# Batch 1 masked by bias products, six half loads, three up products in two parts, and a new instruction order

## The chip, the cores and the metric

The kernel runs on one NeuronCore of one Trainium2 chip. The metric is the device time of one execution in microseconds; seven runs of the kernel before gave a median of 255.86 us (255.72 to 255.92). One further execution was profiled, and every duration below comes from that one.

## The reference, cut to what matters

```python
# q, k, v: 8 batches x 8 heads x 576 positions x 64
rel = pos[:, None] - pos[None, :]
mask_plain = (rel >= 0) & (rel < 32)                        # heads 0 to 3
mask_dil = (rel >= 0) & (rel < 128) & (rel % 4 == 0)        # heads 4 to 7
attn = softmax(where(mask, q @ k.T / 8, -1e9))
x = (attn @ v), heads side by side: 4608 tokens x 512
h = ((x @ w1) * (x @ w2)) @ w3                              # 512 -> 1024 -> 1024
out = h @ w_out                                             # 1024 -> 512, fp32
```

## The kernel before, in words

**Stages.** Each batch is 576 tokens. Attention works on blocks of 96 queries by 128 keys, for four heads at once: a batch has 12 blocks, six for each half of the heads (u = 0 and u = 1). Tokens are kept in the order of their residue modulo 4, so that a dilated window becomes a band too. After attention come, for units of 288 tokens (two per batch, 16 in all), eight pairs of up products (w1 and w2), their elementwise product, and for every 128 tokens a down product with wf = w3 @ w_out, which the kernel computes once.

**Names of the steps.** The kernel puts every step on a list under a name, with the engine, a guessed duration, what it depends on and a rank. The names are used throughout, with batch and part as numbers:

- T: stream transposes on VectorE (DVE) that turn the loaded rows of q, k and v. VT: TensorE transposes of v back to rows (line 403). VK: their copy out of PSUM into the v tile vp (lines 413 and 415).
- S: the score matmuls of one group of blocks (line 445). E: the exp of the group on ScalarE (ACT, line 456). M: its two multiplications by the 0/1 mask on DVE (line 464).
- V: the product with v (line 481) for three blocks, V0.0 to V0.3 in batch 0. R and N: reciprocal and normalisation on DVE (lines 492 and 504). X: TensorE transposes of the result (line 521). K: the copy of X into XT, the operand of the up products (line 529).
- W3T, W3C, W3M, W3D: transpose of a w3 tile (line 638), its copy (645), its product with w_out (650), and the copy into wf (661 and 663).
- A and B: up products with w1 and w2, four matmuls each (line 553). CA: copy of A on ACT (564). G: the product A times B on DVE (569). Y and CY: down product (580) and its copy (591).

**Two ways to mask.** A plain group holds five blocks (40 score matmuls), and its exp is multiplied by the mask afterwards. A biased group holds three blocks: four matmuls of 288 columns (line 428) first write a bias of 0 or -30000 into PSUM, 24 score matmuls add to it, and no M follows. In the kernel before only batch 0 is biased (`BIASED = 1`).

**The order.** The function Plan.run plays the list through with the guessed durations and issues each engine's instructions in the order so found; on the chip nothing is reordered afterwards. Among ready steps of one engine the lowest rank goes first; RANK (FIRST for batch 0) gives the ranks by kind. FIRST_LOADS is the order of the loads after batch 0's, `ON_DVE` names the copies that go to DVE instead of ACT, and LEAD says how far attention runs ahead of the ups. Until the first up product, wherever the plan has no work for TensorE, it puts a filler in: a matmul of 256 columns on zeros (line 692). WARM such matmuls, of 512 columns in the kernel before, stand at the very start (line 675).

**PSUM.** It is used as eight banks. A group of scores takes four (0 to 3 or 4 to 7), a V two, everything else one. A step may start on a bank once the readers of what was there have ended.

**Loads.** q and k of batch 0, u = 0, come whole through SyncE's queue and are rounded on ACT (line 271). All other loads convert to bf16 and are issued by GpSimd (POOL) in one list: rows of q, k and v (line 245), w1 and w2 in three column parts (line 303), w_out (309), w3 (318). At most eight of them are under way, so each issue from the ninth on waits for the landing of the one eight places before. The five mask instructions on POOL (line 358) stand in the same list.

Of the kernel before, what the change touches and what calls it, by code (L numbers as in the profile page):

```python
# [10 lines left out]
P = 128  # L11
BF16 = mybir.dt.bfloat16
F32 = mybir.dt.float32
U32 = mybir.dt.uint32
AL = mybir.AluOpType
# [4 lines left out]
S = 576  # L20
# [8 lines left out]
BIG = 30000.0  # L29
BIASED = 1  # L30
LATE = False
# [3 lines left out]
RES = (0, 2, 1, 3)  # L35
RANK = dict(E=0.4, VK=2, K=0.3, N=1.5, T=3, VT=0.3, S=0.4, V=0.05, X=0.2, W=6, C=-1)
FIRST = {"E": 2, "VK": 0.4, "K": 0.5, "N": 0.2, "T": 2, "VT": 0.05, "S": 0.2, "V": 0.05, "X": 0.4}
WARM = 14
FILL = 110
FIRST_LOADS = ("30", "31", "w0", "w1", "32", "w2", "o0", "o1", "q1", "k1", "33", "34", "v1", "35", "36", "37")  # L40
SHIFT = {}
ON_DVE = ("VK0.0.1", "VK1.0.1", "W3D1", "W3D3", "W3D7")
GRP = 5
WHOLE = ("qn", "kn")
BUSY = 4500
LEAD = 1.1

# [12 lines left out]
class Plan:  # L60
# [15 lines left out]
    def run(self):  # L76
        fills = []
        users = {id(t): [] for t in self.tasks}
# [40 lines left out]
        while len(order) < n:  # L119
            progress = True  # L120
            while progress:
                progress = False
                for e in engines:
# [21 lines left out]
                    if e == "DMA":  # L145
                        free[e] = now + t.dur[0]
                        if t.dur[1]:
                            dma = max(dma, now + t.dur[0]) + t.dur[1]
                            t.end = dma + 1900
                        else:  # L150
                            t.end = free[e]
                    else:
                        t.end = free[e] = now + t.dur
                        if e == "SP" and t.name[0] == "X" and dma > now:
                            t.end = free[e] = now + t.dur + BUSY
                            dma += 1.5 * t.dur
# [23 lines left out]
def kernel(  # L180
# [48 lines left out]
    vts = [const.tile([P, 2, PADK + S, 2], BF16, name=f"vt{i}") for i in range(1)]  # L229
    warm = const.tile([P, 512], BF16, name="warm")  # L230

# [122 lines left out]

    def masks_of_bias():

        for at, first, n in ((0, 0, 4), (4, 1, 2), (6, 4, 3), (9, 4, 3), (12, 0, 4)):
            nc.gpsimd.tensor_scalar(
                out=mask[:, at : at + n, :],
                in0=bias[:, first : first + n, :],  # L360
                scalar1=0.0,
                scalar2=None,
                op0=AL.is_ge,
            )

# [41 lines left out]

    def v_keep(b, u, half, eng):
        dst = vps[b % 2][:, 4 * u : 4 * u + 4, 3 * half : 3 * half + 3, 0:D]
        o = dst.rearrange("p h m (j c) -> p m h j c", c=2)  # L410
        i = spread[(b, u, half)].rearrange("p m c (h j) -> p m h j c", h=4)
        if eng == "ACT":
            nc.scalar.copy(out=o, in_=i)
        else:
            nc.vector.tensor_copy(out=o, in_=i)
# [50 lines left out]
    class Step:  # L466
# [59 lines left out]

        def keep(self, eng):
            if eng == "ACT":
                nc.scalar.copy(out=self.cols(), in_=self.x)
            else:  # L530
                nc.vector.tensor_copy(out=self.cols(), in_=self.x)

# [16 lines left out]

    def up(k, f, w_sb, key):  # L550
        o = bank(UNIT)
        for j, c in enumerate(ORDER):
            nc.tensor.matmul(  # L553
                out=o,
                lhsT=w_sb[:, c, f * P : (f + 1) * P],
                rhs=unit_cols(k, c),
                start=(j == 0),
                stop=(j == DCH - 1),
            )
        held[(key, k, f)] = o  # L560

# [110 lines left out]
    def warm_up():  # L672
        o = bank(512)
        for i in range(WARM):
            nc.tensor.matmul(out=o, lhsT=warm[:, 0:P], rhs=warm, start=True, stop=True)
# [15 lines left out]
    def fill():  # L691
        nc.tensor.matmul(out=bank(256), lhsT=warm[:, 0:P], rhs=warm[:, 0:256], start=True, stop=True)  # L692

# [3 lines left out]
    c0 = add("const2", "DVE", 1400, [c1], constants, -98)  # L697
    add("warm", "PE", 700 + 427 * WARM, [c1], warm_up, 0)

# [45 lines left out]
    plan.dma = 1200 + 1350 * len(WHOLE)  # L745
    for u in range(2):
        for nm in ("qn", "kn", "vn"):
            if u or nm not in WHOLE:
                loads_rows(nm, 0, (u,))
    idt = add("ident", "DMA", (600, 0), [], lambda: make_identity(nc, ident), 2.5, lat=150)  # L750
    bnd = add("band", "DMA", (800, 0), [c1], band, 1.5, lat=150)
    blk = add("blocks", "ACT", 1200, [bnd], blocks, -5, lat=100)
    blk = add("no halo", "DVE", 150, [blk], no_halo, 0, lat=80)
    mk = add("masks", "DMA", (2500, 0), [blk], masks_of_bias, 26.5, lat=150)
    lw12 = {}
    for x in FIRST_LOADS:
# [9 lines left out]
        else:  # L766
            loads_rows(x[0] + "n", c)

# [14 lines left out]
    kept, paced = {}, []  # L783
    prev = {"x": [None] * 4}
    readers, grp_of, todo, n_grp, steps = {}, {}, [], 0, 0
# [24 lines left out]
    for b in range(B):  # L810
# [9 lines left out]
        for u in range(2):  # L820
# [3 lines left out]
            for half in range(2):  # L824
# [3 lines left out]
                if (b, u, half) == (0, 1, 1):  # L828
                    late.append(x)
                name = f"VK{b}.{u}.{half}"  # L830
                eng, dur = ("DVE", 980) if name in ON_DVE else ("ACT", 880)
                vals[(b, u, half)] = [
                    add(name, eng, dur, [x, c0], lambda b=b, u=u, h=half, e=eng: v_keep(b, u, h, e),
                        10 * b + rank("VK", b), lat=100)
                ]
        if b >= DIRECT_V:
# [7 lines left out]
        def group(blocks, biased):  # L844
# [11 lines left out]
            else:  # L856
# [4 lines left out]
                ms = [  # L861
                    add(f"M{n}.{h}", "DVE", 150 + 100 * g.n, [e, mk], lambda h=h: g.masks(h),
                        10 * b + 2, lat=80)
# [21 lines left out]
        while steps < 4 * B:  # L885
# [18 lines left out]
            rc = add(f"R{n}", "DVE", 240, [vv], st.recip, 10 * bb + rank("N", bb), lat=0,  # L904
                     after=[prev["x"][i]])
            ns = [
# [4 lines left out]
            if bb < TURNED:  # L911
                x = add("X" + n, "PE", 310, ns + [idt], st.back, bb - 99 + rank("X", bb), slot=1)
                name = f"K{n}"
                eng, dur = ("DVE", 460) if name in ON_DVE else ("ACT", 640)
                x = add(name, eng, dur, [x], lambda st=st, eng=eng: st.keep(eng),
                        10 * bb + rank("K", bb), lat=100)
            else:
                x = add("XD" + n, "SP", 1300, ns, st.back_dma, 0, lat=1200)
            kept.setdefault(bb, []).append(x)
            prev["x"][i] = x  # L920
            vdone.setdefault(bb, []).append(vv)

# [94 lines left out]
```

## Time and profile before

| | |
|---|---|
| median of 7 runs | 255.86 us |
| the profiled execution | 255.84 us |
| its span in the profile | 254.1 us |
| TensorE busy | 246.8 us (97%), 2763 matmuls |
| DVE busy | 165.5 us (65%) |
| ACT busy | 126.2 us (50%) |
| POOL busy | 66.5 us (26%) |
| fillers | 37, first at 6.8 us, last at 21.4 us |
| granted TensorE clock | 1.00 in every stage asked for |

The span is the time from the first instruction to the last; the 1.7 us between it and the execution's time lie around it. A busy TensorE counts fillers and warm-up as busy. Matmuls overlap, so that the listed duration of one (286 ns for 288 columns) is longer than what it costs; the distance between two starts (about 122 ns) is the cost. Where the text speaks of a wait of TensorE, it means that the next matmul in its fixed order was not yet ready.

### The profile page before, as it was taken

How to read it: one execution, taken by the hardware profiler on the slowest of the kernel's cores; microseconds unless marked ns; L12 is line 12 of the kernel's file. 1: busy time of each engine (PE TensorE's matmuls, PEld its weight loads, DVE VectorE, ACT ScalarE, POOL GpSimd, SP SyncE). 2: the span in 40 equal slices, each digit the busy share in tenths (PEclk: the TensorE clock that was granted, in tenths of full speed). 3: DMA queues.
4: the chain of work that ended last, by engine and by line, in shares of the span. 5: the costliest groups of instructions: out<-in, count | busy, mean ns of one | idle time of the engine just before them, and what ended most of it. 6: DMA issues, size and time to landing. Idle time of an engine off the chain costs nothing.

```text
span 254.1 us, 6809 instructions
## 1 busy us (share of the span) xinstructions
PE 246.8 (97%) x2763; PEld 170.1 (67%) x2763; DVE 165.5 (65%) x342; ACT 126.2 (50%) x221; POOL 66.5 (26%) x103
## 2 busy tenths in 40 slices
PE   7799999999999999999999999999999999999994
PEld 2588766565777666667676766776767666777662
DVE  3983547799889898678767886837737365333321
ACT  5677333986635534463636626356353553333331
POOL 7653129643622712008160310700000000000000
PEclk9999999999999999999999999999999999999999
DMA  7999999999999999828999658852332222311114
GB/s 225 207 199 206 207 211 210 209 103 189 185 136 182 205 186 171 193 67 140 167 143 160 95 72 106 120 100 67 67 65 67 66 68 67 102 33 56 42 41 124
DMA packets 59374, 33.40 MB, mean 131 GB/s; under 512 B 44752, under 2 KB 49232, under 8 KB 59344
## 3 DMA queue, kind: packets, MB, share of 16 engines
q0 software_dynamic: 38544, 18.81, 58.2%
q1 hardware_dynamic: 20656, 14.10, 23.2%
q8 instruction: 21, 0.34, 0.6%
q14 instruction: 9, 0.07, 0.1%
q10 hardware_dynamic: 144, 0.07, 0.1%
HBM read 38.80 MB, written 9.44 MB: 190 GB/s over the span
## 4 chain that ended last, share of the span: by engine, by line
PE 93%; ACT 3%; DMA 2%; DVE 1%; issue 0%; ACTq 0%
PE ps L553 50%; PE ps L580 24%; PE ps L650 5%; PE ps L481 4%; PE ps L445 4%; DMA gt<-in_q_dram 2%; ACT et L456 2%; PE ps L692 2%; PE ps L638 1%; PE ps L403 1%; PE ps L521 1%; ACT w3T L645 1%; PE ps L598 1%; DVE qt L394 1%; ACT qn L271 0%; DVE kt L379 0%
## 5 line engine op out<-in xcount | busy, mean ns | idle before, releaser
L553 PE MATMUL ps<-XT,w_sb 128*128 128x288 bf16 x1024 | 136.2, 286 | 0.0
L553 PEld LDWEIGHTS <-w_sb 128*128 128x128 bf16 x1024 | 97.8, 98 | 30.6
L569 DVE TENSOR_TENSOR gt<-ps,asb 128x288 bf16<-128x288 f32 x128 | 57.6, 454 | 52.0 <-PE ps L553 49.8
L564 ACT CAST asb<-ps 128x288 bf16<-128x288 f32 x128 | 51.1, 400 | 51.7 <-PE ps L553 49.4
L580 PE MATMUL ps<-wf_sb,gt 128*128 128x512 bf16 x280 | 65.8, 379 | 0.0
L591 ACT COPY osb<-ps 128x512 f32<-128x512 f32 x35 | 20.5, 587 | 56.3 <-PE ps L580 56.3
L580 PEld LDWEIGHTS <-gt 128*128 128x128 bf16 x280 | 27.4, 98 | 26.9
L293 POOL DMA_DIRECT2D vp<-in_v_dram x48 | 30.0, 635 | 38.3 <-PE ps L481 21.7
L456 ACT ACTIVATE et<-ps 128x1920 bf16<-128x1920 f32 (+2 forms) x21 | 34.2, 1635 | 5.5 <-PE ps L445 4.9
L504 DVE TENSOR_TENSOR xo<-ps,rcp 96x384 bf16<-96x384 f32 (+1 forms) x48 | 31.5, 676 | 0.6
L464 DVE TENSOR_TENSOR et<-et,mask 128x960 bf16<-128x960 bf16 (+1 forms) x34 | 21.4, 645 | 4.9 <-ACT et L456 4.7
L394 DVE STREAM_TRANSPOSE qt<-qn 128x320 uint32<-128x320 uint32 (+3 forms) x34 | 22.4, 669 | 2.1 <-ACT qn L271 1.8
L481 PEld LDWEIGHTS <-et 128*128 128x128 bf16 x384 | 14.3, 98 | 1.7
L481 PE MATMUL ps<-vp,et 128*128 128x65 bf16 x384 | 15.1, 193 | 0.0
L650 PE MATMUL ps<-wo_sb,w3T 128*128 128x512 bf16 x64 | 14.8, 379 | 0.1
L394 DVE STREAM_TRANSPOSE kt<-kn 128x320 uint32<-128x320 uint32 (+3 forms) x18 | 11.6, 642 | 4.4 <-PE ps L445 4.3
L492 DVE RECIPROCAL rcp<-ps 96x12 f32<-96x12 f32 x32 | 6.8, 215 | 10.5 <-PE ps L481 10.2
L245 POOL DMA_DIRECT2D kn<-in_k_dram x8 | 5.5, 686 | 30.4 <-DVE kt L394 18.4
L445 PEld LDWEIGHTS <-kt 32*128 32x128 bf16 x768 | 9.1, 92 | 6.3 <-issue 4.5
L445 PE MATMUL ps<-qt,kt 32*128 32x96 bf16 x768 | 12.1, 201 | 1.2 <-DVE kt L379 1.2
L379 DVE STREAM_TRANSPOSE kt<-kn 128x576 uint32<-128x576 uint32 (+1 forms) x9 | 9.9, 1121 | 1.4 <-PE ps L445 1.4
L650 PEld LDWEIGHTS <-w3T 128*128 128x128 bf16 x64 | 5.9, 98 | 6.8 <-ACT w3T L645 0.6
(55 smaller groups left out, 119.1 us busy)
## 6 DMA issues: line engine op xcount, KB each, us to landing
qn<-in_q_dram POOLq DMA_DIRECT2D x7, 576.0 KB, 8.1
kn<-in_k_dram POOLq DMA_DIRECT2D x7, 576.0 KB, 7.4
w3n<-in_moe_w_dram POOLq DMA_DIRECT2D x8, 256.0 KB, 15.1
out_dram<-osb SPq DMA_DIRECT2D x7, 256.0 KB, 2.5
out_dram<-osb SPq DMA_DIRECT2D x8, 224.0 KB, 2.9
vp<-in_v_dram POOLq DMA_DIRECT2D x6, 288.0 KB, 9.8
out_dram<-osb SPq DMA_DIRECT2D x8, 192.0 KB, 2.7
out_dram<-osb SPq DMA_DIRECT2D x8, 160.0 KB, 3.5
```

The source lines that it names most:

```text
L293: nc.gpsimd.dma_start(out=vp[32 + p0 : 32 + p0 + n, 4:8, m, 0:D], in_=v_rows(b, 4, 4 * t0 + res, [[4 * D, n], [S * D, 4], [1, D]]),)
L394: nc.vector.transpose(out=o, in_=i)
L445: nc.tensor.matmul(out=self.sp[:, g, QB * i : QB * i + QB], lhsT=kt[prt, u, QB * m : QB * m + P, c], rhs=qq, start=(c == 0 and not biased) ...
L456: nc.scalar.activation(out=ev, in_=self.sp[:, :, 0:x], func=ACT.Exp, scale=scale)
L464: nc.vector.tensor_tensor(out=ev, in0=ev, in1=mk, op=AL.mult)
L481: nc.tensor.matmul(out=self.o[:, g, mm, :], lhsT=grp.et[:, c0 : c0 + P], rhs=vps[self.b % 2][:, 4 * self.u + g, 3 * self.hf + mm, 0 : D + ...
L504: nc.vector.tensor_tensor(out=dst, in0=self.o[0:QB, hs, :, 0:D], in1=self.rcp[0:QB, hs, :].unsqueeze(3).to_broadcast([QB, n, 3, D]), op=AL ...
L553: nc.tensor.matmul(out=o, lhsT=w_sb[:, c, f * P : (f + 1) * P], rhs=unit_cols(k, c), start=(j == 0), stop=(j == DCH - 1),)
L564: nc.scalar.copy(out=a_sb, in_=held[("a", k, f)])
L569: nc.vector.tensor_tensor(out=gt[:, f, c0 : c0 + UNIT].rearrange("p (r m t) -> p m r t", r=2, m=BLK), in0=held[("b", k, f)].rearrange("p ( ...
L580: nc.tensor.matmul(out=y, lhsT=gt[:, f, c0 : c0 + P], rhs=wf_sb[:, f, :], start=(f == 0), stop=(f == KFF - 1),)
L650: nc.tensor.matmul(out=o, lhsT=w3T[ft][:, g, :], rhs=wo_sb[:, g, :], start=(g == 0), stop=(g == KFF - 1),)
```

## The change

- Batch 1 is biased too (`BIASED = 2`): its blocks form four groups of three with bias products, and have no mask multiplications. The groups of five begin with batch 2.
- Batch 1's q, k and v are loaded in two halves each (u = 0, u = 1), six loads for three, at new places in FIRST_LOADS. Batch 0's four loads on POOL get their own order (B0_LOADS), and w1 and w2 come ahead of most of w3.
- The first three up products (A0.0, B0.0, A0.1) are two tasks each: the two matmuls on the first heads' half (XT0), and later the two on the second (XT1).
- Six copies (HALVED: K1.0, K1.1, VK0.0.0, VK1.0.1, VK1.1.0, VK1.1.1) are two instructions, half on ACT and half on DVE. Some other copies move between the two engines (ON_DVE).
- The mask instructions are five tasks at an earlier place in POOL's list.
- The warm-up is 28 matmuls of 256 columns for 14 of 512.
- Ranks and LEAD have new values, and the plan's model of the loads knows of the limit of eight. By these the instruction order of every engine changes in most places; the number of instructions changes little: TensorE gets 16 bias matmuls more and 17 fillers fewer (20 for 37), DVE four mask multiplications fewer.

The new order on TensorE, by the names above, from the start to the first ups (each V, S and VT as a whole; "p" is the first part of an up product):

```
warm-up, filler, S0.0, S0.1, filler, VT0.0 (both halves), 7 fillers, V0.0, S0.2, VT0.1.0,
3 fillers, X0.0, V0.1, filler, S0.3, 4 fillers, V0.2, X0.1, VT0.1.1, W3T0, 2 fillers,
A0.0p, X0.2, B0.0p, filler, V0.3, A0.0, A0.1p, B0.0, A0.1, B0.1, A0.2, ...
```

and in batch 1's stage:

```
A1.7, W3M0, W3T2, W3M1, W3T3, W3M2, VT1.0, W3T4, W3M3, W3M4, S1.0, S1.1, V1.0, W3T5, B1.7, V1.1,
VT1.1, W3T6, W3M5, X1.0, W3T7, W3M6, S1.2, S1.3, V1.2, X1.1, W3M7, V1.3, X1.2, Y0, S2.0, X1.3, A2.0, ...
```

The diff, cut to its core:

```diff
 BIG = 30000.0
-BIASED = 1
+BIASED = 2
 LATE = False
 TURNED = 2
 DIRECT_V = 2
 ORDER = (2, 3, 0, 1)
 RES = (0, 2, 1, 3)
-RANK = dict(E=0.4, VK=2, K=0.3, N=1.5, T=3, VT=0.3, S=0.4, V=0.05, X=0.2, W=6, C=-1)
-FIRST = {"E": 2, "VK": 0.4, "K": 0.5, "N": 0.2, "T": 2, "VT": 0.05, "S": 0.2, "V": 0.05, "X": 0.4}
-WARM = 14
+RANK = dict(E=0.2, VK=0.2, K=1, N=1, T=0.3, VT=0.05, S=0.4, V=0.2, X=0.4, W=0.5, C=5)
+FIRST = {"E": 0.5, "VK": 0.2, "K": 3, "N": 0.3, "T": 1.5, "VT": 0.05, "S": 0.3, "V": 0.2, "X": 0.05}
+WARM = 28
 FILL = 110
-FIRST_LOADS = ("30", "31", "w0", "w1", "32", "w2", "o0", "o1", "q1", "k1", "33", "34", "v1", "35", "36", "37")
+FIRST_LOADS = ("w0", "30", "w1", "w2", "o0", "31", "o1", "32", "33", "v10", "34", "q10", "k10", "q11", "35", "v11", "36", "k11", "37")
 SHIFT = {}
-ON_DVE = ("VK0.0.1", "VK1.0.1", "W3D1", "W3D3", "W3D7")
+ON_DVE = ("K0.2", "K1.0", "K1.1", "K1.3", "VK1.0.1", "VK1.1.0", "W3D0", "W3D3", "W3D4", "W3D6")
 GRP = 5
 WHOLE = ("qn", "kn")
+B0_LOADS = ("k1", "v0", "q1", "v1")
+HALVED = ("K1.0", "K1.1", "VK0.0.0", "VK1.0.1", "VK1.1.0", "VK1.1.1")
+MASK_AT = 19.5
+PARTED = 3
 BUSY = 4500
-LEAD = 1.1
+LEAD = 1.3
 
...
                         if t.dur[1]:
-                            dma = max(dma, now + t.dur[0]) + t.dur[1]
+                            if len(landed) >= 8:
+                                free[e] = max(now, landed[-8]) + t.dur[0]
+                            dma = max(dma, free[e]) + t.dur[1]
                             t.end = dma + 1900
+                            landed.append(t.end)
                         else:
...
 
-    def masks_of_bias():
-
-        for at, first, n in ((0, 0, 4), (4, 1, 2), (6, 4, 3), (9, 4, 3), (12, 0, 4)):
-            nc.gpsimd.tensor_scalar(
-                out=mask[:, at : at + n, :],
-                in0=bias[:, first : first + n, :],
-                scalar1=0.0,
-                scalar2=None,
-                op0=AL.is_ge,
-            )
+    MASKS = ((0, 0, 4), (4, 1, 2), (6, 4, 3), (9, 4, 3), (12, 0, 4))
+
+    def mask_of_bias(i):
+
+        at, first, n = MASKS[i]
+        nc.gpsimd.tensor_scalar(
+            out=mask[:, at : at + n, :],
+            in0=bias[:, first : first + n, :],
+            scalar1=0.0,
+            scalar2=None,
+            op0=AL.is_ge,
+        )
 
...
 
-    def v_keep(b, u, half, eng):
+    def v_keep(b, u, half, eng, hs=slice(0, 4)):
         dst = vps[b % 2][:, 4 * u : 4 * u + 4, 3 * half : 3 * half + 3, 0:D]
-        o = dst.rearrange("p h m (j c) -> p m h j c", c=2)
-        i = spread[(b, u, half)].rearrange("p m c (h j) -> p m h j c", h=4)
+        o = dst.rearrange("p h m (j c) -> p m h j c", c=2)[:, :, hs, :, :]
+        i = spread[(b, u, half)].rearrange("p m c (h j) -> p m h j c", h=4)[:, :, hs, :, :]
         if eng == "ACT":
...
 
-        def keep(self, eng):
+        def keep(self, eng, c=slice(0, 6 * QB)):
             if eng == "ACT":
-                nc.scalar.copy(out=self.cols(), in_=self.x)
+                nc.scalar.copy(out=self.cols()[:, c], in_=self.x[:, c])
             else:
-                nc.vector.tensor_copy(out=self.cols(), in_=self.x)
+                nc.vector.tensor_copy(out=self.cols()[:, c], in_=self.x[:, c])
 
...
 
-    def up(k, f, w_sb, key):
-        o = bank(UNIT)
-        for j, c in enumerate(ORDER):
+    def up(k, f, key, chunks=ORDER, first=True, last=True):
+        if first:
+            held[(key, k, f)] = bank(UNIT)
+        for j, c in enumerate(chunks):
             nc.tensor.matmul(
-                out=o,
-                lhsT=w_sb[:, c, f * P : (f + 1) * P],
+                out=held[(key, k, f)],
+                lhsT={"a": w1_sb, "b": w2_sb}[key][:, c, f * P : (f + 1) * P],
                 rhs=unit_cols(k, c),
-                start=(j == 0),
-                stop=(j == DCH - 1),
+                start=(first and j == 0),
+                stop=(last and j == len(chunks) - 1),
             )
-        held[(key, k, f)] = o
 
...
     def warm_up():
-        o = bank(512)
+        o = bank(256)
         for i in range(WARM):
...
     def fill():
-        nc.tensor.matmul(out=bank(256), lhsT=warm[:, 0:P], rhs=warm[:, 0:256], start=True, stop=True)
+        nc.tensor.matmul(out=bank(256), lhsT=warm[:, 0:P], rhs=warm, start=True, stop=True)
 
     plan.fill, plan.fill_from = fill, 2000
 
     c1 = add("const", "DVE", 1200, [], first_constants, -99)
     c0 = add("const2", "DVE", 1400, [c1], constants, -98)
-    add("warm", "PE", 700 + 427 * WARM, [c1], warm_up, 0)
+    add("warm", "PE", 700 + 213 * WARM, [c1], warm_up, 0)
 
...
     plan.dma = 1200 + 1350 * len(WHOLE)
-    for u in range(2):
-        for nm in ("qn", "kn", "vn"):
-            if u or nm not in WHOLE:
-                loads_rows(nm, 0, (u,))
+    for x in B0_LOADS:
+        loads_rows(x[0] + "n", 0, (int(x[1]),))
     idt = add("ident", "DMA", (600, 0), [], lambda: make_identity(nc, ident), 2.5, lat=150)
     bnd = add("band", "DMA", (800, 0), [c1], band, 1.5, lat=150)
     blk = add("blocks", "ACT", 1200, [bnd], blocks, -5, lat=100)
     blk = add("no halo", "DVE", 150, [blk], no_halo, 0, lat=80)
-    mk = add("masks", "DMA", (2500, 0), [blk], masks_of_bias, 26.5, lat=150)
+    mk = [
+        add(f"masks{i}", "DMA", (x, 0), [blk], lambda i=i: mask_of_bias(i), MASK_AT + 0.1 * i,
+            lat=150)
+        for i, x in enumerate((1200, 710, 940, 940, 1200))
+    ]
     lw12 = {}
...
         else:
-            loads_rows(x[0] + "n", c)
+            loads_rows(x[0] + "n", c, (int(x[2]),) if x[2:] else None)
 
...
                 eng, dur = ("DVE", 980) if name in ON_DVE else ("ACT", 880)
+                ways = [(eng, dur, slice(0, 4))]
+                if name in HALVED:
+                    ways = [("ACT", 540, slice(0, 2)), ("DVE", 560, slice(2, 4))]
                 vals[(b, u, half)] = [
-                    add(name, eng, dur, [x, c0], lambda b=b, u=u, h=half, e=eng: v_keep(b, u, h, e),
+                    add(name, e, dur, [x, c0],
+                        lambda b=b, u=u, h=half, e=e, hs=hs: v_keep(b, u, h, e, hs),
                         10 * b + rank("VK", b), lat=100)
+                    for e, dur, hs in ways
                 ]
...
                 eng, dur = ("DVE", 460) if name in ON_DVE else ("ACT", 640)
-                x = add(name, eng, dur, [x], lambda st=st, eng=eng: st.keep(eng),
+                ways = [(eng, dur, slice(0, 6 * QB))]
+                if name in HALVED:
+                    ways = [("ACT", 400, slice(0, 3 * QB)), ("DVE", 270, slice(3 * QB, 6 * QB))]
+                x = [
+                    add(name, e, dur, [x], lambda st=st, e=e, c=c: st.keep(e, c),
                         10 * bb + rank("K", bb), lat=100)
+                    for e, dur, c in ways
+                ]
             else:
-                x = add("XD" + n, "SP", 1300, ns, st.back_dma, 0, lat=1200)
+                x = [add("XD" + n, "SP", 1300, ns, st.back_dma, 0, lat=1200)]
             kept.setdefault(bb, []).append(x)
             prev["x"][i] = x
             vdone.setdefault(bb, []).append(vv)
 
-    seq = 10
+    seq, parted = 20, 0
     G, Y, gates, stores, pairs = {}, {}, [], [], []
 
     def ups(k, f):
         nonlocal seq
         b, hf = k // 2, k % 2
-        need = kept[b][0:2] + kept[b][2 + hf : 3 + hf]
+        plain = kept[b][0] + kept[b][1]
+        need = plain + kept[b][2 + hf]
         wl = lw12[(0, 0, 1, 1, 2, 2, 2, 2)[f]]
         lap = k * UNIT - RING
         free = [Y[i] for i in range(max(0, lap // P), (lap + UNIT - 1) // P + 1)]
-        seq += 1
-        a = add(f"A{k}.{f}", "PE", 490, need + wl, lambda: up(k, f, w1_sb, "a"), seq, slot=1,
-                after=free + pairs[-1:])
+
+        def product(key, after):
+
+            nonlocal seq, parted
+            name = f"{key.upper()}{k}.{f}"
+            seq += 1
+            if k or parted == PARTED:
+                return add(name, "PE", 490, need + wl, lambda: up(k, f, key), seq, slot=1,
+                           after=after), []
+            parted += 1
+            p = add(name + "p", "PE", 245, plain + wl,
+                    lambda: up(k, f, key, ORDER[2:], last=False), seq - 5, slot=1, after=after)
+            return add(name, "PE", 245, need + [p],
+                       lambda: up(k, f, key, ORDER[:2], first=False), seq), [p]
+
+        a, p = product("a", free + pairs[-1:])
         pairs.append(a)
-        ca = add("CA", "ACT", 400, [a], lambda: copy_a(k, f), -1, lat=100,
+        ca = add("CA", "ACT", 400, [a] + p, lambda: copy_a(k, f), -1, lat=100,
                  after=[gates[-6] if len(gates) > 5 else None])
-        seq += 1
-        bb = add(f"B{k}.{f}", "PE", 490, need + wl, lambda: up(k, f, w2_sb, "b"), seq,
-                 slot=1, after=[a])
-        G[(k, f)] = add("G", "DVE", 460, [bb, ca], lambda: gate(k, f), -1, lat=100)
+        bb, p = product("b", p or [a])
+        bb = [bb] + p
+        G[(k, f)] = add("G", "DVE", 460, bb + [ca], lambda: gate(k, f), -1, lat=100)
         gates.append(G[(k, f)])
```

More of the change, by code (lines that the diff above doesn't have):

```diff
@@ L76, in run @@
     def run(self):
-        fills = []
+        fills, landed = [], []
         users = {id(t): [] for t in self.tasks}
@@ L229 @@
     vts = [const.tile([P, 2, PADK + S, 2], BF16, name=f"vt{i}") for i in range(1)]
-    warm = const.tile([P, 512], BF16, name="warm")
+    warm = const.tile([P, 256], BF16, name="warm")
     def bank(n, dtype=F32):
@@ L783 @@
     kept, paced = {}, []
-    prev = {"x": [None] * 4}
+    prev = {"x": [[]] * 4}
     readers, grp_of, todo, n_grp, steps = {}, {}, [], 0, 0
@@ L861, in group @@
                 ms = [
-                    add(f"M{n}.{h}", "DVE", 150 + 100 * g.n, [e, mk], lambda h=h: g.masks(h),
+                    add(f"M{n}.{h}", "DVE", 150 + 100 * g.n, [e] + mk, lambda h=h: g.masks(h),
                         10 * b + 2, lat=80)
@@ L904 @@
             rc = add(f"R{n}", "DVE", 240, [vv], st.recip, 10 * bb + rank("N", bb), lat=0,
-                     after=[prev["x"][i]])
+                     after=prev["x"][i])
             ns = [
```

## The prediction

> **What bounds the kernel now.** I read the page first, then TensorE by stage, then its instructions in order of time.
>
> ```profile
> span 254.1 us, 6809 instructions
> PE 246.8 (97%) x2763; PEld 170.1 (67%) x2763; DVE 165.5 (65%) x342; ACT 126.2 (50%) x221; POOL 66.5 (26%) x103
> ```
>
> The busy time by stage (us from:to, length, then TensorE's busy time first):
>
> ```profile
> 0.00:6.90 6.90, 5.37 (x15) 2.03 (x16) 2.65 (x19) 4.11 (x9) 5.58 (x17) 1.00 0.76 224
> 6.90:21.70 14.80, 12.93 (x258) 10.81 (x257) 11.36 (x26) 10.67 (x14) 7.90 (x12) 1.00 1.25 203
> 21.70:61.70 40.00, 39.85 (x460) 27.60 (x459) 28.04 (x51) 24.35 (x38) 16.89 (x24) 1.00 1.20 188
> 61.70:250.40 188.70, 188.66 (x2036) 129.69 (x2034) 123.16 (x249) 86.84 (x162) 36.17 (x53) 1.00 0.72 111
> ```
>
> From 21.7 to 250.4 us TensorE stands still for 0.19 us in all. A DVE, ACT or DMA instruction saved there is worth nothing; a matmul added costs its time. What can be gained lies before 21.5 us, where much of "busy" is filler. The timeline (start, duration) of TensorE's last start-up steps:
>
> ```profile
> 15.84 0.43 PE L521 MATMUL ps<-ident,xo 96*128 96x96 bf16 x6
> 16.11 1.80 PE L692 MATMUL ps<-warm 128*128 128x256 bf16 x15
> 17.75 0.65 PE L428 MATMUL ps<-bias,ident 128*128 128x288 bf16 x4
> 18.33 0.44 PE L445 MATMUL ps<-qt,kt 32*128 32x96 bf16 x24
> 18.70 0.51 PE L403 MATMUL ps<-ident,vt 128*128 128x128 bf16 x6
> ...
> 19.31 1.80 PE L692 MATMUL ps<-warm 128*128 128x256 bf16 x15
> 20.95 0.53 PE L481 MATMUL ps<-vp,et 128*128 128x65 bf16 x12
> 21.32 0.38 PE L692 MATMUL ps<-warm 128*128 128x256 bf16 x2
> 21.53 1.63 PE L553 MATMUL ps<-XT,w_sb 128*128 128x288 bf16 x12
> ```
>
> Durations overlap; starts give the cost. A filler is 0.109 us (1.64/15); a biased score group 0.95 (17.75 to 18.70); the up products begin at 21.53. A group of five plain blocks costs 0.65: the four ups from 64.81 need 0.49 of the 1.14 to 65.95.
>
> ```profile
> 64.81 0.65 PE L553 MATMUL ps<-XT,w_sb 128*128 128x288 bf16 x4
> 65.40 0.62 PE L445 MATMUL ps<-qt,kt 32*128 32x96 bf16 x40
> 65.95 1.16 PE L553 MATMUL ps<-XT,w_sb 128*128 128x288 bf16 x8
> ```
>
> Loads land one by one; POOL's waits for the ninth and later issues show when:
>
> ```profile
> 7.88 0.75 POOL L303 DMA_DIRECT2D w_sb<-in_moe_w_dram  x1 [0.30 <-DMA vn<-in_v_dram]
> 9.37 0.74 POOL L303 DMA_DIRECT2D w_sb<-in_moe_w_dram  x1 [0.74 <-DMA qn<-in_q_dram]
> 10.76 0.54 POOL L318 DMA_DIRECT2D w3n<-in_moe_w_dram  x1 [0.64 <-DMA kn<-in_k_dram]
> 12.11 0.74 POOL L303 DMA_DIRECT2D w_sb<-in_moe_w_dram  x1 [0.81 <-DMA vn<-in_v_dram]
> ```
>
> So POOL's first four half loads land at about 7.9, 9.3, 10.7 and 12.0 us.
>
> **What the Trainium skill says.** "TensorE: Matmul & The Clock Gate", section "Wait — 56ns, not 53.3ns?": start to start N/2.4 GHz plus 2.5 ns when warm, N/1.2 GHz cold. The trace agrees: 16 ups in 1.96 us are 122.5 ns for N=288, and the first warm-up matmuls of 512 columns stand 426 ns apart. "PSUM — Partial Sum Buffer", section "PSUM bank collisions raise a hardware error": two engines may not even read one bank together. So a copy "in halves on two engines" out of one bank is one half after the other; no bank of the kernel before is read that way, so no trace shows it yet. The same page, "Engine vs sequencer instructions": ACT and DVE queues are strict FIFO and matmuls start in program order, so a late instruction holds all behind it; the trace shows nothing against it.
>
> **The change, part by part.**
>
> *Bias for batch 1: on the path.* Batch 1's twelve blocks become four biased groups of three; plain groups go from 16 of five and one of four to 14 of five and one of two. Four times 0.95, less 2 x 0.65, less about 0.22 for the two blocks fewer in the last group: **+2.3 us** of TensorE. In return DVE drops four mask multiplies, about 3 us of DVE. That is hidden: TensorE never waited for DVE after 21.7. ACT's exps stay even (four of 1.13 for two of 1.77 and a shorter last one).
>
> *Start-up: load order, fillers, parted ups.* POOL's first four loads become k, v, q, v (were v, q, k, v), then w1/w2's first columns, which were seventh and eighth and are now fifth and sixth: they land by 15 us instead of 17.5. Fillers fall from 37 to 20. I walk the new order with the durations above. Nothing moves until S0.1 ends at 10.1. DVE then does three k parts (0.39, 0.35, 0.39 start to start) from 8.57 before v's transpose, 9.71 to 10.95, so VT0.0 starts at 11.0 (10.46 before). VK0.0.0's DVE half runs 11.54 to 12.05, its ACT half after it to 12.53: V0.0 at 12.58, where seven fillers have ended at 12.42. From there TensorE's own list: V0.0 0.37, biased S0.2 0.95, VT 0.35, three fillers 0.33, X0.0 0.26, V0.1 0.37, a filler 0.11, biased S0.3 0.95 (to 16.27), four fillers 0.44, V0.2 0.37, X0.1 0.26, VT 0.35, W3T0 0.45, two fillers 0.22, A0.0's first part 0.24 at 18.36, X0.2 0.26, B0.0's 0.24, a filler, V0.3 0.37: the rest of A0.0 at 19.6, or 19.7 with the waits for N0.2 (X0.2 at 18.66) and K0.2. ACT keeps pace: E0.2 14.02, VK0.1.0 15.09, K0.0 15.79, E0.3 16.4, K0.1 17.4, VK0.1.1 ends 18.8, with V0.3 due at 19.3. By then four up matmuls are done (0.49) and eight w3 transposes fewer (0.45): even. **-1.85 us** against 21.53. From below it can hardly be more than 2.1 (that list without a wait); from above it shrinks with each late step.
>
> *The other orders, K and VK halves, masks.* Ups then run without a gap as before: w1's second columns land near 18.7 and are needed at 21, w2's by 24 and needed at 27. In batch 1's stage TensorE's order is S1.0, S1.1, V1.0 and later S1.2, S1.3, V1.2. An exp starts 1.07 after its group's first bias matmul and takes 1.13, so V1.0 is ready 2.25 after S1.0 began, while the two groups take 1.9: TensorE waits 0.35, twice, with W3T5 and X1.1 queued behind. Y0's bank waits for W3D7: 0.15. Before, this stage (36 to 61.7) had about 0.6 of such waits (47.05 to 47.39 the longest). **+0.25 us**, 0 to +1. Masks move on POOL (4.76 us, off the path) ahead of k of batch 1, whose half I put at 38.5 with DVE wanting it at 44: hidden while it is less than 5 us late. K1.0, K1.1 and VK1.x in serial halves are hidden by a W3 product (1.73) that runs meanwhile; without it they would cost about 0.1 each. From 63 us to the end, both orders are ups, downs and five-block groups without TensorE waits: 0, at worst a few tenths. WARM in 256-column pieces is the same 7168 columns, ending before S0.0's wait for k at 8.78: 0.
>
> Sum: 2.3 - 1.85 + 0.25 = **+0.7 us** on the profiled execution, whose 254.1 span stands for 255.84 us, as good as the median 255.86: 256.5.
>
> **Rivals.** *Not slower: the batch 1 stage pays for the bias.* The chain of waits between 43.7 and 47.3 runs over ACT (a w3T copy 1.01, a 1920-column exp 1.67, a w3T copy 0.92); shorter exps and no masks may free TensorE of its 0.6 us there and add no new wait. Then 2.3 - 1.85 - 0.6 = -0.15: 255.7; with the start-up at its bound of 2.1, 255.4, and below 255.3 if v's transpose comes earlier than walked. It decides if V1.0 and V1.2 follow within 0.1 us of the scores. For it: ACT carries that chain. Against it: exp after scores is 2.25 us by rows of this trace. *Slower still: v lands late.* Batch 0's v is now POOL's second load, at 9.3 with DVE ready at 9.71. Up to 0.4 us late costs nothing; beyond, VT0.0, V0.0 and ACT's chain from E0.2 to VK0.1.1 move one for one, and DMA queues are loaded throughout (share 1.25). One transfer late (1.4) costs 1.0: 257.5. Against it: same sizes, same issue times. *The change does nothing it says:* the masks' removal is such a case already (worth 0); the rest is in the instruction order and cannot fail to be there.
>
> **Numbers.** Measurement tells about 0.2% (0.5 us) from no change: 255.35 to 256.37. The forecast has 0.50 (its own range 256.0 to 257.0: 0.14 in "same", 0.36 slower), the first rival 0.32 (0.14 same, 0.18 faster, as its start-up term is open), late v 0.18. Faster 0.18, same 0.28, slower 0.54. Range 255.2 to 257.6.
>
> **What would show it.** Right: first up matmul near 18.4 and an unbroken run from 19.7; two waits of 0.3 to 0.4 at V1.0 and V1.2; 32 bias matmuls of 0.12; no TensorE idle after 63. Wrong: ups unbroken only after 20.5 (late v, or halves that cost more), before 19.3, or TensorE waits over 1.5 us between 36 and 63.

## The result and the profile after

The changed kernel took 256.47 us (median of 13 runs, 256.42 to 256.70) where the kernel before took 255.84 (median of 31): a ratio of 1.0025, 95% interval 1.0018 to 1.0032. It is 0.63 us slower, against 0.7 forecast. Medians are over all executions; the ratios leave out those over 1.5% longer than the fastest of their kernel (among the experiments three of 14, two of 14, one of 6 and two of 22). The profiled execution took 256.60 us. The top of its page:

```profile
span 254.8 us, 6842 instructions
PE 247.1 (97%) x2776; PEld 171.6 (67%) x2776; DVE 165.0 (65%) x345; ACT 124.7 (49%) x222; POOL 68.3 (27%) x106
```

The span grew by 0.7 us and TensorE's count by 13 matmuls. Busy shares say nothing: they are what they were. The table by stage, with the columns of before, says where to look:

```profile
6.90:21.70 14.80, 12.76 (x250) 10.15 (x249) 13.30 (x30) 10.41 (x14) 6.80 (x11) 1.00 1.27 203
21.70:61.70 40.00, 39.41 (x444) 26.76 (x442) 25.86 (x49) 22.82 (x37) 22.40 (x33) 1.00 1.18 185
61.70:250.40 188.70, 188.70 (x2052) 130.13 (x2051) 122.66 (x248) 86.99 (x162) 33.48 (x48) 1.00 0.74 111
```

TensorE is idle for 0.59 us between 21.7 and 61.7 (0.15 before) and not at all from there to 250.4. So the difference is made before 61.7 us, by when the ups begin and by what batch 1's stage holds. TensorE's start-up in order of time (start, duration, and idle time before with its releaser):

```profile
10.95 0.84 PE L412 MATMUL ps<-ident,vt 128*128 128x128 bf16 x12 [0.32 <-DVE vt L388]
11.64 0.93 PE L701 MATMUL ps<-warm 128*128 128x256 bf16 x7
12.69 0.53 PE L490 MATMUL ps<-vp,et 128*128 128x65 bf16 x12
...
18.45 0.41 PE L563 MATMUL ps<-XT,w_sb 128*128 128x288 bf16 x2
...
19.31 0.53 PE L490 MATMUL ps<-vp,et 128*128 128x65 bf16 x12
19.68 2.61 PE L563 MATMUL ps<-XT,w_sb 128*128 128x288 bf16 x20
```

The first part of an up product is at 18.45, V0.3 at 19.31, and the unbroken ups start at 19.68: 1.85 us sooner than 21.53. In batch 1's stage (same columns) the two V groups that follow biased scores wait for their exp:

```profile
45.73 0.65 PE L437 MATMUL ps<-bias,ident 128*128 128x288 bf16 x4
...
46.69 0.66 PE L437 MATMUL ps<-bias,ident 128*128 128x288 bf16 x4
...
47.99 0.54 PE L490 MATMUL ps<-vp,et 128*128 128x65 bf16 x12 [0.26 <-ACT et L465]
...
54.95 0.65 PE L437 MATMUL ps<-bias,ident 128*128 128x288 bf16 x4
...
57.21 0.54 PE L490 MATMUL ps<-vp,et 128*128 128x65 bf16 x12 [0.27 <-ACT et L465]
```

From the start of the ups to the end of the span the kernel before needs 254.1 - 21.53 = 232.57 us, the changed one 254.8 - 19.68 = 235.12. So what follows the start-up, with the bias in it, costs 2.55 us more, the start-up pays 1.85 back, and 0.7 remains. (The profiled execution lies 0.13 above the median, and in several of the experiments' profiles the same steps of the start-up stand about that much earlier.)

### The profile page after: what moved, and what is told of

It reads as the page before. It is cut to its first block, busy times and chain, and to the rows that moved or that the text cites. A ratio compares the mean times of both kernels' runs of the same rounds, so it can differ in the third digit from the quotient of the medians.

```text
span 254.8 us, 6842 instructions
## 1 busy us (share of the span) xinstructions
PE 247.1 (97%) x2776; PEld 171.6 (67%) x2776; DVE 165.0 (65%) x345; ACT 124.7 (49%) x222; POOL 68.3 (27%) x106
## 4 chain that ended last, share of the span: by engine, by line
PE 92%; DVE 2%; ACT 2%; DMA 2%; issue 0%; ACTq 0%; DVEq 0%
PE ps L563 50%; PE ps L589 24%; PE ps L659 5%; PE ps L490 5%; PE ps L454 4%; DMA gt<-in_q_dram 2%; PE ps L647 1%; ACT et L465 1%; PE ps L412 1%; PE ps L437 1%; PE ps L530 1%; DVE qt L403 1%; PE ps L607 1%; PE ps L701 1%; ACT qn L278 0%; DVE kt L403 0%
## 5 line engine op out<-in xcount | busy, mean ns | idle before, releaser
L300 POOL DMA_DIRECT2D vp<-in_v_dram x48 | 30.2, 636 | 53.9 <-PE ps L490 24.2
L473 DVE TENSOR_TENSOR et<-et,mask 128x960 bf16<-128x960 bf16 (+1 forms) x30 | 18.5, 632 | 4.2 <-ACT et L465 4.1
L286 POOL DMA_DIRECT2D vp<-in_v_dram x6 | 7.7, 1285 | 10.6 <-PE ps L490 9.8
L252 POOL DMA_DIRECT2D qn<-in_q_dram x9 | 5.9, 654 | 13.2 <-DVE qt L403 10.4
```

The costliest lines, as they stand in the source:

```text
L300: nc.gpsimd.dma_start(out=vp[32 + p0 : 32 + p0 + n, 4:8, m, 0:D], in_=v_rows(b, 4, 4 * t0 + res, [[4 * D, n], [S * D, 4], [1, D]]),)
```

## The experiments

**The theory** is the prediction's: bias products are TensorE time on the path (+2.3, and +0.25 of waits), and an earlier first up product pays most of it back. **The rivals:** batch 1's stage is bound by something else, so that the products cost little; the start-up gain comes from the order of the weight loads; or it comes from one of the small edits (parted ups, halved copy) alone. The experiments ran on three chips, on which the kernel before took 255.79, 255.83 and 255.84 us; where a run is compared with the changed kernel's 256.47, differences of 0.05 us or less are not told apart.

### Bias products of batch 1 left out, order kept

```diff
         def scores(self, biased=False):
             self.sp = ps[:, plan.now.place : plan.now.place + 4, :]
+            biased = biased and self.blocks[0][0] == 0
```

The 16 bias matmuls of batch 1 are gone, so its masking isn't done; every other instruction keeps its place.

> The changed kernel without the 16 bias products of batch 1 (its scores stay unmasked); every other instruction in the same order. The forecast's terms: 16 products of 0.122 are 1.96 us of TensorE, but half of them are covered: S1.0 and S1.1 then take 0.92 instead of 1.9, while V1.0 still waits for the exp, which starts 0.49 after its scores and takes 1.13, so that its wait grows from 0.3 to about 0.75, and V1.2's too. Net -1.0, 255.4 to 255.6 us. If the bias were paid for by the stage altogether (the first rival), nothing changes: 256.4 to 256.6. If nothing covers it, -1.95: 254.5.

Measured: 255.50 us (median), ratio to before 0.9993 (0.9980 to 1.0007). Leaving out 16 matmuls, which with the change to the score matmuls take TensorE 4 x 0.58 us (46.31 - 45.73), gave back 0.97 us, as expected. Its TensorE timeline in the stage shows what came in their place:

```profile
46.71 0.42 PE L455 MATMUL ps<-qt,kt 32*128 32x96 bf16 x21 [0.56 <-DVE wf_sb L673]
47.35 0.54 PE L491 MATMUL ps<-vp,et 128*128 128x65 bf16 x12 [0.22 <-ACT et L466]
...
55.25 0.44 PE L455 MATMUL ps<-qt,kt 32*128 32x96 bf16 x24 [0.41 <-DVE wf_sb L673]
56.08 0.54 PE L491 MATMUL ps<-vp,et 128*128 128x65 bf16 x12 [0.39 <-ACT et L466]
```

The second group of each pair now waits for the bank that a W3D copy is still reading (0.56 and 0.41), and V still waits for its exp (0.22 and 0.39). The expectation had a longer wait for the exp alone; its sum was right, the bank it had not seen. In the changed kernel the second group begins with its bias matmuls, at 46.69, and no wait for a bank is listed there. So in this order somewhat under half of the products is what the time shows; the rest of the 2.55 stays when the products go. It fits the order that the biased groups bring, two pairs of groups, each with a V close behind; no run tries that order by itself.

### The changed kernel with only batch 0 biased

```diff
-BIASED = 2
+BIASED = 1
```

> The changed kernel with batch 1 masked by multiplications again (BIASED = 1), all else as changed; start-up order and its 20 fillers stay as they are, the later order follows from the plan. Forecast's terms: the bias term of 2.3 and the two waits for exps (0.25 more than before) go: 253.9 us (253.6 to 254.3), 0.8% faster than before. First rival (the stage pays for the bias): 256.2 to 256.6.

Measured: 259.71 us (259.11 to 259.83), ratio 1.0145 (1.0127 to 1.0163): almost 6 us off what I expected. The start-up was as fast as expected (the unbroken ups begin at 19.52); the loss is later. Waits of TensorE (us in total, times, longest):

```profile
PE ps L659 <- ACT w3T L654: 1.7, 1, 1.7
...
PE ps L454 <- ACT et L465: 1.3, 1, 1.3
PE ps L563 <- ACT et L465: 1.2, 1, 1.2
```

The expectation took a value of a constant for the removal of instructions. Plan.run makes a new order from it, and with plain groups and the new ranks, loads and LEAD that order is bad: a W3M stands directly behind its w3T copy, which stands on ACT behind a five-block exp of 1.77 us. TensorE idles 2.34 us between 40 and 61.7 and 2.50 us between 61.7 and 100 (busy 19.36 of 21.70 and 35.80 of 38.30). Which of the constants does it was not separated.

### The kernel before with batch 1 biased

```diff
-BIASED = 1
+BIASED = 2
```

> The kernel before with BIASED = 2 and nothing else; its start-up with 37 fillers stays. Forecast's terms: +2.3 for the bias and up to 0.3 for waits on exps: 258.2 us (257.9 to 258.5). First rival: 255.7 to 256.1.

Measured: 259.10 us (258.88 to 260.18), ratio 1.0134 (1.0114 to 1.0154), so +3.3 us. The direction and most of the size are those of the theory. Of the excess of 0.7, about 0.3 lies outside the span: the spans of its five runs are 256.7 to 257.1 (median 257.0, 3.0 above the 254.0 of the runs of before beside it), and why three of them took 0.2 to 1.5 us more around the span than the usual 1.8 is open. Within the span the rest fits the replanned order: all four biased groups stand in a row at 43.13 to 47.4, and TensorE is idle 0.75 us between 40 and 61.7 for exps, a w3T copy and the banks behind them.

### The first three ups whole, at the place of their second part

```diff
-            p = add(name + "p", ..., lambda: up(k, f, key, ORDER[2:], last=False), ...)
+            p = add(name + "p", ..., reserve, ...)        # takes the bank, no matmul
-            return add(name, ..., lambda: up(k, f, key, ORDER[:2], first=False), seq), [p]
+            return add(name, ..., whole, seq), [p]        # all four matmuls
```

> The changed kernel with the three parted up products whole again, all four matmuls at the place of the second part, every other instruction in the same order. Forecast's terms: the six first-part matmuls no longer run ahead; four of them (0.49 us) stood among start-up steps where TensorE then only waits for N0.2 and K0.2: +0.4 to +0.5, 256.9 to 257.0 us. Rival: the start-up is bound elsewhere and they filled nothing: 256.4 to 256.6.

Measured: 256.93 us (256.87 to 257.02), 0.46 more than with parted ups. The four early matmuls (0.49) fill places where TensorE would stand idle; the runs show no other effect of the parting.

### VK0.0.0 as one copy on ACT

```diff
     def v_keep(b, u, half, eng, hs=slice(0, 4)):
+        if (b, u, half) == (0, 0, 0):
+            if eng == "DVE":
+                return
+            hs = slice(0, 4)
```

> The changed kernel with VK0.0.0 as one copy on ACT (0.80 us) in place of a DVE half and an ACT half out of the same bank; all else in the same order. In the trace of the changed kernel the DVE half runs 11.57 to 12.13 and the ACT half only after it, to about 12.6. If halves of one bank run one after the other, the whole copy starts at 11.5 and ends at 12.3: V0.0 follows its fillers at 12.4 instead of 12.69, and DVE's next steps come 0.47 earlier: 0.1 to 0.3 us faster, 256.2 to 256.4. If halves were really parallel, the whole copy would cost up to 0.3: 256.7 to 256.8.

Measured: 256.18 us, 0.29 less. From the timelines, first the two halves of the changed kernel, then the whole copy and the V0.0 that reads it (both ACT rows hold the next copy as well):

```profile
11.57 0.56 DVE L424 COPY vp<-ps 128x384 bf16<-128x384 bf16 x1
```

```profile
12.16 1.18 ACT L422 COPY vp<-ps 128x384 bf16<-128x384 bf16 x2 [0.82 <-DVE vp L424]
```

```profile
11.38 1.50 ACT L426 COPY vp<-ps 128x768 bf16<-128x768 bf16 x2
```

```profile
12.28 0.53 PE L494 MATMUL ps<-vp,et 128*128 128x65 bf16 x12
```

ACT's half starts when DVE's ends, with DVE named as the releaser, as the prediction took from the Trainium skill ("PSUM — Partial Sum Buffer", section "PSUM bank collisions raise a hardware error"). The halves also start 0.19 us later than the whole copy, since DVE is still at a transpose of q until 11.49. V0.0 comes at 12.69 with halves; with the whole copy it follows its seven fillers at 12.28. Of these 0.41 us, 0.12 lie ahead of the edit (VT0.0 at 10.83 for 10.95), and the other 0.29 is what the time shows. So halving this copy costs time; the other five halved copies were not tried alone.

### Two w3 loads ahead of w1 and w2

```diff
     order, _ = plan.run()
+    # on POOL's list: LW3.0 and LW3.1 moved ahead of the first w1/w2 load
```

> The changed kernel with the first two w3 loads ahead of w1 and w2 again, as in the kernel before; only POOL's order of loads differs. w1/w2's first columns then land near 17.5 and are wanted at 18.4, the second near 20.1 and wanted at 20.9, the third by 25.3 and wanted at 27: nothing, 256.4 to 256.6 us. If the earlier weights carry the start-up gain, the first up product waits: +0.5 or more.

Measured: 256.47 us (256.38 to 256.68), the same as the changed kernel. The first ups are not held by their weights at this distance, so the new order of the weight loads isn't where the 1.85 us come from.

### Batch 0's first v a place later on POOL

```diff
     order, _ = plan.run()
+    # on POOL's list: the load of v (u = 0) and that of q (u = 1) change places
```

> The changed kernel with batch 0's v (u = 0) and q (u = 1) loads exchanged in POOL's order, so that v lands third (10.7) instead of second (9.3). The second rival's price, by the prediction's walk: DVE wants v at 9.65, so VT0.0 starts near 12.0 instead of 10.95 and the rest of the start-up moves with it: +0.8 to +1.1, 257.3 to 257.6 us. If start-up is not bound by this chain: under +0.3.

Measured: 257.35, 257.38 and 257.49 us in three runs, and 258.67, 258.74 and 259.94 in three others; the ratio over all is 1.0091 (1.0063 to 1.0120). The first three are +0.9 to +1.0, as expected. The profile was taken in the 258.67 run, and its TensorE timeline shows a second cost:

```profile
11.70 1.31 PE L412 MATMUL ps<-ident,vt 128*128 128x128 bf16 x12 [1.11 <-DVE vt L388]
12.81 1.70 PE L701 MATMUL ps<-warm 128*128 128x256 bf16 x7
14.30 0.86 PE L490 MATMUL ps<-vp,et 128*128 128x65 bf16 x12
```

Seven fillers take 1.49 us from start to start, 0.213 each where a filler cost 0.109: TensorE runs at half rate. The table of windows says so too, with a granted clock (third number from the end) of 0.50:

```profile
8.49:11.90 3.41, 1.88 (x57) 1.20 (x58) 2.62 (x7) 2.15 (x2) 1.58 (x3) 1.00 1.19 202
11.90:15.31 3.41, 3.41 (x33) 2.85 (x31) 1.94 (x6) 1.18 (x2) 1.91 (x3) 0.50 1.33 201
15.31:18.72 3.41, 3.41 (x87) 2.63 (x86) 3.26 (x7) 2.51 (x4) 1.04 (x3) 1.00 1.39 201
```

VT0.0 is 0.75 late, and it, the fillers, V0.0 and the bias of S0.2 take 0.42, 0.73, 0.31 and 0.16 longer; less 0.28 us of waiting that V0.0 had anyway, the ups are 2.1 us late, and start at 21.75. Ahead of the half rate stands a stretch of waits: 1.65 us before S0.0, 0.26 and 1.11 after it. The mean granted clock that is listed for each run tells the two groups apart: 0.999 or 1.00 for the three at 257.4, 0.993, 0.993 and 0.984 for the others.

### The fillers left out

```diff
     def fill():
-        nc.tensor.matmul(out=bank(256), lhsT=warm[:, 0:P], rhs=warm, start=True, stop=True)
+        pass
```

> The changed kernel without the 20 fillers of the start-up (warm-up stays). They fill real waits, apart from some 0.3 us: ACT's chain E0.2, VK0.1.0, K0.0, E0.3, K0.1, VK0.1.1 is packed from 14.1 to 19.0 and sets V0.3. So 0.1 to 0.4 us faster, 256.1 to 256.4. Rival: the fillers keep the matmul clock up, and without them matmuls slow down: slower by 0.5 or more.

Measured: 256.09 us, 0.38 less than with fillers, ratio to before 1.0004 (0.9993 to 1.0014). Of 20 x 0.109 = 2.18 us of fillers only that much stands in the way of work; the rest lies in waits. The rival, slower matmuls without fillers, shows in none of the 12 runs of 14 that lie at 256.01 to 256.12. Of the other two, the profiled one (260.14) keeps the full clock and loses its time between 90 and 97 us; the other (266.85) has no profile.

### The new start-up with the old constants for the rest

```diff
-BIASED = 2
+BIASED = 1
-RANK = dict(E=0.2, ...)       # and LEAD, MASK_AT:
+RANK = dict(E=0.4, ...)       # all as in the kernel before
-FIRST_LOADS = ("w0", "30", "w1", "w2", ...)   # and ON_DVE: as in the kernel before,
+FIRST_LOADS = ("w0", "30", "w1", "31", ...)   # but for w0, w1 and batch 0's copies
-HALVED = ("K1.0", "K1.1", "VK0.0.0", "VK1.0.1", "VK1.1.0", "VK1.1.1")
+HALVED = ("VK0.0.0",)
```

FIRST, B0_LOADS, the parted ups and the model of the loads stay as in the change, and so do the early first loads of w1 and w2 and the engines of batch 0's copies.

> The new start-up alone: the changed kernel with BIASED = 1, and with batch 1's loads, masks, ranks, LEAD and copies as in the kernel before; only batch 0's load order, the early w1/w2, FIRST, the three parted products and VK0.0.0 in halves stay (20 fillers, same TensorE order up to the first ups as the changed kernel). Forecast's term: -1.85 against before, if the order that the plan then finds for batch 1's stage waits no more than before's 0.6 us: 254.0 us, and 254.6 with 0.6 us more of waits. Rival: the bias is needed to make use of the early start, and without it the stage waits for exps and copies of w3 as in the run with BIASED = 1: 255.5 or more.

Measured: a median of 255.04 us with one run at 253.98 and the others from 254.66 up, ratio 0.9957 (0.9942 to 0.9972). The median is above what I expected, and still below the rival's 255.5; the lowest run is 1.86 below the kernel before, as much as the start-up was forecast to gain, but it is a single run. The profile (255.25 us) shows one reason why others aren't there:

```profile
8.70 0.44 PE L454 MATMUL ps<-qt,kt 32*128 32x96 bf16 x24 [2.12 <-DVE kt L388]
...
11.89 1.70 PE L701 MATMUL ps<-warm 128*128 128x256 bf16 x7
```

The seven fillers are at half rate again, and the ups start at 20.86. In this execution the warm-up was over at 5.82 us (6.60 in the profile of the changed kernel), so the wait for k was longer. The half rate accounts for this run and may be part of the slowest one (258.73); both list a mean clock of 0.993. The runs at 254.66, 255.00 and 255.07 list 0.999 or 1.00; by that they did not fall, and why they are late is open.

### The same without fillers and with VK0.0.0 whole

> The kernel of the new start-up alone, further without fillers and with VK0.0.0 as one ACT copy. By the runs that did each of these alone on the changed kernel (-0.3 and -0.38) up to 0.6 us below the start-up alone: 253.5 to 254.1 if that is 254.0; at worst the same as it.

Measured: 253.45 us (median; four runs at 253.27 to 253.58, two at 254.26 and 254.31), ratio 0.9914 (0.9898 to 0.9930). It beats both kernels: 0.86% under the one before, 1.2% under the changed one. The last two rows of its start-up:

```profile
18.33 0.53 PE L494 MATMUL ps<-vp,et 128*128 128x65 bf16 x12
18.80 1.39 PE L567 MATMUL ps<-XT,w_sb 128*128 128x288 bf16 x10
```

The parts add up: 253.98 - 0.29 (whole copy) - 0.38 (no fillers) = 253.31, with the single lowest run of the last experiment to start from. The same two edits, if their effects add, would put the changed kernel at 256.47 - 0.67 = 255.80; that kernel was not run. By this estimate biasing batch 1, with the constants that come with it, costs 2.35 us (against the median) to 2.5, where 2.55 was forecast.

### The kernel before without its fillers

> The kernel before without its 37 fillers. Of its start-up the prediction says that 17 fillers fewer are what the new order gains. In before, S0.3's operands are ready at 16.6 while fillers hold it to 17.75. Without them ACT sets the pace: K0.1 to 18.1, E0.3 then (18.82 before), VK0.1.1 to 19.9, V0.3 at 20.0 (20.95 before): -0.9 to -1.0, 254.8 to 255.0 us. If fillers only filled real waits: 255.7 to 255.9. If the clock needs them: slower.

Measured: a median of 256.35 us, spread in two groups: eight runs from 255.04 to 255.70, most others from 256.2 to 257.8; ratio 1.0012 (0.9996 to 1.0028). The better group is 0.1 to 0.8 below the kernel before, in the middle 0.6, where I expected 0.9 to 1.0. The profiled run (257.62) shows two losses:

```profile
20.78 3.04 PE L553 MATMUL ps<-XT,w_sb 128*128 128x288 bf16 x12
...
94.13 3.10 PE L553 MATMUL ps<-XT,w_sb 128*128 128x288 bf16 x24 [0.84 <-DMA XT<-xo]
```

The ups begin at 20.78, but the first twelve take 2.83 us, to 23.61, where 1.47 is their time at full rate: the granted clock is 0.50 from 20.55 to 23.96. And at 94.13 TensorE waits for a part of XT that a DMA transpose brings; the profiles of the kernel before and of the changed one have no such wait. Nine of these 22 runs list a mean clock of 0.993 or less, one of the 27 runs of the kernel before beside them. So the fillers of the kernel before cost something and also hold the clock; taking them out is a gain only where the waits left behind are short.

## Why the prediction was right

**The start-up term, -1.85, is measured at -1.85.** The walk met the trace nearly line by line: VT0.0 11.0 for 10.95, V0.0 12.58 for 12.69, the first up 18.36 for 18.45, X0.2 18.66 for 18.70, V0.3 19.3 for 19.31, the unbroken ups 19.7 for 19.68. (The first figure of each pair is the forecast.) There is a little luck in the last pair: V0.0 came 0.11 later than walked, and the 0.1 of waits for N0.2 and K0.2 did not come. The experiments say in part what the term consists of: the parted ups bring 0.46, the halved copy loses 0.29, the earlier weight loads do nothing. If these effects add, the order of batch 0's steps and loads, with 17 fillers fewer in it, brings the remaining 1.68 (1.85 + 0.29 - 0.46). Within it, the order of the loads, the ranks and the fillers were not separated; the 20 fillers that are left still cost 0.38.

**The bias term, +2.3, with +0.25 of waits, is measured at 2.55 in sum.** The parts hold too, if waits are read, as the prediction did, from distances between starts (the listed idle begins only at the modelled end of the matmul before). The group pitch was 0.96 (45.73 to 46.69), against 0.95. V1.0 and V1.2 start 2.26 us after the first bias matmul of their pair (45.73 to 47.99, 54.95 to 57.21), against 2.25; less two pitches, that is a wait of 0.34 each, against 0.35, of which 0.26 and 0.27 are listed. Y0 waits 0.2, against 0.15. The kernel before had these waits in the stage, of which the list shows 0.15:

```profile
43.64 0.62 PE L445 MATMUL ps<-qt,kt 32*128 32x96 bf16 x40
44.19 0.62 PE L638 MATMUL ps<-ident,w3n 128*128 128x128 bf16 x8
44.81 1.90 PE L650 MATMUL ps<-wo_sb,w3T 128*128 128x512 bf16 x8
46.64 0.61 PE L445 MATMUL ps<-qt,kt 32*128 32x96 bf16 x40
47.39 1.90 PE L650 MATMUL ps<-wo_sb,w3T 128*128 128x512 bf16 x8
```

The eight w3 transposes cost 0.45 where nothing holds what follows, so 0.17 of the 0.62 to 44.81 is a wait; the five-block group took 0.55 to 44.19 and 0.75 to 47.39, so 0.20 is one (from 47.19; the prediction has it begin too early, at 47.05). With 0.18 before 50.89 and 0.07 before 54.53 they make the 0.6 of the prediction. The waits thus grew by 0.3, and 2.25 is left for the products and all else.

Read as a cause, the term was too simple: with the products left out and the order kept, only 0.97 came back, since W3D's banks and the exps then held TensorE instead. The sum holds as a comparison of two whole orders (the last but one experiment gives an estimate of 2.35 to 2.5), not as a price of 16 matmuls.

**Costs put at nothing.** There was no TensorE idle from 61.7 to 250.4; the weight loads had room; the new place of the mask instructions was not tried alone, and no wait of TensorE in the changed kernel leads to them.

**The rivals.** The stage did not pay for the bias: V1.0 and V1.2 waited 0.34 us for their exps and did not follow within 0.1 us of the scores, which was that rival's condition. v was not late: VT0.0 waited 0.32 us and was where the walk put it. Its price of 1.0 for one transfer was right at full rate (0.9 to 1.0), but the rival lacked the half rate that such a wait can bring, 1.2 us more; with it the case would have ended above the range. That the changed kernel's own waits bring no half rate (none of its 13 runs lists a mean clock under 0.997) is luck as far as the prediction goes: it did not ask what waits do to the clock.

**The expectations did worse than the prediction.** Two of them (batch 0 alone biased in the changed kernel, both batches biased in the one before) priced an edit of one constant by the instructions it adds or removes. The plan turns such an edit into another order, worth up to 6 us. The prediction was spared that because it walked the order that was really issued.

## What to carry to other kernels

When a scheduler makes the order, price the order and not the edit: write down the new sequence of the bounding engine and walk it with durations of the old trace. An instruction on the bounding engine is worth its duration only if what follows it is ready by then; ask which bank or operand is late next before counting its removal. Don't expect a copy out of one PSUM bank to gain from being split over two engines (here it lost 0.29 us), and test work that only fills waits both ways, since it may cost time (0.38 in the changed kernel) and also hold the clock.

## What the runs showed of the hardware

TensorE fell to half rate after waits shorter than I would have thought to matter. A filler of 256 columns took 0.213 us instead of 0.109 after waits of 2.12, 0.26 and 0.17 us in one run, and of 1.65, 0.26 and 1.11 within 4.7 us in another; 3.41 us later it was at full rate again. The Trainium skill ("TensorE: Matmul & The Clock Gate", Part 1) has the half rate (256 columns at 1.2 GHz are 0.213 us, as measured) and a free-running window of about 3.4 us that decides it; it asks for a window of idle time, where here a window that was idle for two thirds or less of its length sufficed.

The traces agree with a free-running window. In the three profiles that fell, the warm-up reached full rate at 4.19, 5.07 and 6.90 us, and the half rate began at 11.02, 11.90 and 20.55: 6.83, 6.83 and 13.65 us later, which is two, two and four times 3.41. In each, the granted clock is 0.50 for 3.41 us. Where the steps fall against this grid changes from run to run, which is a likely reason why one kernel falls in some executions only. An early grid also ends the warm-up early (5.82 and 6.24 us in two of the three, against 6.60 in the changed kernel's, which held its rate through a wait of 1.33 us), so that the wait for k that follows is longer. How much idle time makes TensorE fall can't be read from these runs: TensorE was idle for 1.4 to 1.5 us in the 3.41 us before each fall, and the changed kernel without fillers had 2.0 us within 3.41 and did not fall.

Half rate for 3.41 us makes a mean granted clock of 0.993 over 254 us, and that is what the three profiled runs list. Late runs that list 0.998 to 1.00 (255.00 us for the new start-up alone, 257.53 for the kernel before without fillers) would then be late for another reason. The wait for a DMA transpose at 94.13 us is one that a profile shows; for the runs without a profile the cause is open.
